# Loading the first six raw weight pieces from SyncE's queue instead of ScalarE's

## The chip, the cores and the metric

The kernel runs on one core of one Trainium2 chip. The metric is the device time of the whole program in microseconds (us), lower is better. Three runs of the kernel before gave 1136.29, 1137.8 and 1132.78 us; the median is 1136.29 us. All statements on where time goes come from one more execution, taken with the hardware profiler.

## The reference

The program is an attention block followed by two feed-forward blocks. Cut to what matters:

```python
# attention: 4 batches x 8 heads, 576 tokens, head size 64
scores = q @ k.T / 8
scores = where(scores >= max(scores) - tau, scores, -1e9)
attn = exp(scores - max(scores)); attn = attn / (sum(attn) + 1e-9)
x = (attn @ v) laid out as (2304, 512)
# first block: w_in 512 x 2048, w_out 2048 x 512
h = relu(x @ w_in); y = (s * h * h + b) @ w_out
# second block: same sizes, other weights
h2 = y @ w2_in; out = (h2 * tanh(log1p(exp(h2)))) @ w2_out
```

Inputs are float32, but the weights `w_in`, `w_out`, `w2_in` and `w2_out` reach the core as 64-bit floats, read as pairs of 32-bit words, and the kernel puts each number together from the two words itself.

## The kernel before

**Attention** works on 16 pairs of heads (4 batches x 4 pairs). A pair has 9 row tiles of 128 rows (`ti` 0 to 8). For each tile `scores` multiplies (S, L338), finds the maximum (`ns`, VectorE, L342) and takes the exponential (ScalarE, L349); later `weights_t` transposes the result on TensorE (T, L376) and ScalarE copies it out (`te`, L387); `products_v` multiplies with v (pv, L406); `split_x` (L414) cuts the pair's output into two parts, `self.x[pr]`.

The q and k of the next pair are prepared one pair ahead, in `prep_qk` (L294), k at `ti` 2 and q at `ti` 4. `raw_t` transposes the raw tile on TensorE and at once issues the load of the raw tile of the pair after (L250, L251). `parts` (L274) splits the transposed tile into a high part on ScalarE (`hik` or `hiq`, L278) and a low part on VectorE (`lok`, `loq`, L279). k and q share one buffer for the high part and one for the low. **Moves** then copy these parts between partitions into the operand tiles KH, KL and Q, as DMAs of 144 KB on SyncE's queue (L299): six for k, four for q. `self.moved` is the last move issued so far. So `hiq` can be written only when the moves that read `hik` have landed.

**Weight pieces.** `w_in` and `w_out` are cut into 32 pieces of 512 KB of raw words. `split_w` takes one piece through five steps: its load into a raw tile (L59, four buffers); nothing; a scaling on ScalarE in place (L65); three bit operations on VectorE (L67 to L69, two buffers); a rounded copy on ScalarE (L72) and a subtraction (L73). `split_all` starts one piece at each call and moves each live piece by one step. Finished pieces go into `ring` (five buffers) and are stored to DRAM (L194, SyncE's queue), to be read again for later batches. The marks `keep_in_program_order` on L59 and L65 keep these loads and scalings in the order of the program on ScalarE's queue.

`run` calls `split_all` (`next(w1)`) six times while `self.x[3]` doesn't exist yet, at steps 42, 52, 62, 72, 82 and 92 of the attention generator. These calls start pieces 0 to 5. During this stage the PSUM pool `self.s2p` is open; afterwards it is `None`. The remaining 26 pieces are started from `first()`, within the first block's work on batch 0 (`moe1(0)`: h and y, L503), interleaved with attention of pair 4 and on. Step 42 falls in pair 2 at `ti` 2, just after the k moves for pair 3 are traced; steps 52 and 62 come after the q moves for pair 3; steps 72 and 82 after the q moves for pair 4; step 92 after the q moves for pair 5.

**Order.** Each engine has one queue and runs it strictly in order. The order in a queue is set when the program is built, by a planner that simulates a timeline and may put an instruction ahead of others traced before it. A DMA is issued by the engine whose queue it is in: `nc.sync` is SyncE (SP), which does nothing else, and `nc.scalar` is ScalarE (ACT), which also does all the copies and exponentials. An issue that must wait holds up what stands behind it in that queue. `issue_after(i)` ties an instruction of the same engine behind instruction `i`.

Of the kernel before, what the change touches and what calls it, by code (L numbers as in the profile page):

```python
# [19 lines left out]
class Fused:  # L20
# [26 lines left out]
    def split_w(self, src, hi, lo, pool, tags, kw):  # L47

        nc = self.nc
        i = self.nd
        self.nd += 1
        n = src.shape[1] * src.shape[2] // 2
        raw = pool.tile([P, n, 2], I32, tag=tags[0], name=f"wraw{i}", **kw)
        self.tc.keep_in_program_order(nc.scalar.dma_start(raw.rearrange("p (c f) w -> p c (f w)", c=src.shape[1]), src))  # L59
        low, high = raw[:, :, 0], raw[:, :, 1]  # L60
        hf = high.bitcast(F32)
        yield
        yield
        a = pool.tile([P, n], I32, tag=tags[1], name=f"wa{i}")
        self.tc.keep_in_program_order(nc.scalar.activation(hf, hf, AF.Copy, scale=2.0 ** -112))  # L65
        yield
        nc.vector.tensor_scalar(a, high, 3, None, op0=ALU.logical_shift_left)  # L67
        nc.vector.scalar_tensor_tensor(a, low, 29, a, op0=ALU.logical_shift_right, op1=ALU.bitwise_or)
        nc.vector.scalar_tensor_tensor(a, high, -0x80000000, a, op0=ALU.bitwise_and, op1=ALU.bitwise_or)  # L69
        yield  # L70
        af = a.bitcast(F32).rearrange("p (c f) -> p c f", c=src.shape[1])
        nc.scalar.copy(hi, af)  # L72
        (nc.gpsimd if self.s2p else nc.vector).tensor_tensor(lo, af, hi.bitcast(F32), op=ALU.subtract)  # L73
# [863 lines left out]
```

## Time and profile before

| | us |
|---|---|
| median of three runs | 1136.29 |
| lowest, highest of the three | 1132.78, 1137.8 |
| the profiled execution, its own time | 1133.57 |
| its span (first to last instruction) | 1131.8 |
| TensorE (PE) busy | 1081.1 |
| VectorE (DVE) busy | 806.3 |
| ScalarE (ACT) busy | 619.0 |

Lines of a trace read so: start, duration, engine (SPq and ACTq are the issuing queues of SyncE and ScalarE), line of the kernel, operation, tile written <- tiles read, shapes, count, and in square brackets how long the engine sat idle before it and what ended that. Rows on DMA issues give the tile, the count, the size and the median us from issue to landing. Rows of stretches give, for each engine, busy us and the number of instructions, then the granted clock of TensorE as a share of full speed, the mean busy share of the 16 DMA engines, and GB/s.

### The profile page before, as it was taken

To read this page: it belongs to the slowest core of one execution; us is meant where nothing else is said; L and a number is where in the kernel's file an instruction comes from. 1 tells how busy PE (TensorE), PEld (TensorE's weight loads), DVE (VectorE), ACT (ScalarE), POOL (GpSimd) and SP (SyncE) were. 2 spreads that over 40 slices of the span, in tenths; PEclk is the share of its full clock that TensorE was granted. 3 is DMA by queue.
4 is the path that set the end of the run, shared out by engine and by line. 5 is a ranking of instruction groups with operands and counts; after the bars stand their busy time and mean duration, and the time that the engine had idled before them with its cause. 6 is when DMAs were issued, how large, how long until landed. Compare 5 with 4: busy or idle time off the path is not lost.

```text
span 1131.8 us, 21384 instructions
## 1 busy us (share of the span) xinstructions
PE 1081.1 (96%) x7964; PEld 1018.7 (90%) x7964; DVE 806.3 (71%) x1746; ACT 619.0 (55%) x1153; POOL 263.4 (23%) x306
## 2 busy tenths in 40 slices
PE   7887799999999999999999989999999999999998
PEld 6765599898999998888989879999999999999998
DVE  6987799999666677878866666735696368725782
ACT  4655497684576665667747557634363244513351
POOL 4533273351352442325334301100000000000000
PEclk9998899999999999999999999999999999999999
DMA  7366585966847869689864599977998999996683
GB/s 163 80 169 167 172 256 207 300 199 203 246 135 215 249 222 278 214 292 302 310 211 141 190 355 365 361 268 282 351 383 319 343 420 367 348 336 253 263 294 117
DMA packets 141591, 292.70 MB, mean 259 GB/s; under 512 B 52848, under 2 KB 78960, under 8 KB 133168
## 3 DMA queue, kind: packets, MB, share of 16 engines
q1 hardware_dynamic: 123408, 274.26, 70.8%
q10 hardware_dynamic: 18080, 17.07, 5.2%
q8 instruction: 63, 1.03, 0.4%
q14 instruction: 40, 0.33, 0.1%
HBM read 201.85 MB, written 66.58 MB: 237 GB/s over the span
## 4 chain that ended last, share of the span: by engine, by line
PE 67%; DVE 3%; DMA 3%; ACT 2%; issue 1%; POOL 0%; DVEq 0%; ACTq 0%; POOLq 0%
PE o L748 16%; PE y L503 13%; PE h L503 12%; PE qY L614 6%; PE qX L614 4%; PE qV L614 4%; PE S L338 3%; PE pv L406 3%; PE T L376 3%; DMA wso<-chlo 1%; DMA wi<-wsi 1%; PE pv L403 1%; PE T L381 1%; DMA w<-w 1%; ACT e L349 0%
## 5 line engine op out<-in xcount | busy, mean ns | idle before, releaser
L363 POOL TENSOR_SCALAR e<-e,st 128x576 f32<-128x576 f32 x128 | 133.4, 1055 | 229.0 <-DVE st L358 163.9
L748 PE MATMUL o<-wo,hl 128*128 128x256 f32 x1512 | 177.7, 279 | 0.0
L748 PEld LDWEIGHTS o<-wo,hl 128*128 128x128 f32 x1512 | 177.4, 188 | 0.0
L503 PE MATMUL y<-gh,w 128*128 128x288 f32 x768 | 165.0, 300 | 3.4 <-ACT y L548 1.7
L503 PE MATMUL h<-xh,w 128*128 128x288 f32 x768 | 164.7, 299 | 1.6 <-ACT xh L414 0.7
L342 DVE TENSOR_SCALAR_CACHE_REDUCE ns<-S 128x576 f32<-128x576 f32 x144 | 108.0, 752 | 53.6 <-PE S L338 53.2
L349 ACT ACTIVATE e<-ns,st 128x576 f32<-128x576 f32 x128 | 99.1, 776 | 64.4 <-DVE ns L342 62.0
L387 ACT COPY te<-T 128x576 f32<-128x576 f32 x144 | 91.8, 637 | 72.4 <-PE T L381 61.7
L353 DVE SCALAR_TENSOR_TENSOR e<-ns,st,e 128x576 f32<-128x576 f32 x128 | 114.9, 899 | 22.6 <-ACT e L349 21.6
L503 PEld LDWEIGHTS y<-gh,w 128*128 128x128 f32 x768 | 126.7, 189 | 4.5 <-ACT y L548 2.0
L503 PEld LDWEIGHTS h<-xh,w 128*128 128x128 f32 x768 | 125.8, 188 | 2.9 <-ACT xh L414 1.2
L527 POOL TENSOR_TENSOR gl<-rr,gh 128x288 fp32r<-128x288 f32 x96 | 93.6, 989 | 128.8 <-ACT rr L526 128.8
L503 PE MATMUL y<-gl,w 128*128 128x288 f32 x384 | 113.9, 297 | 0.9 <-POOL gl L527 0.9
L503 PE MATMUL h<-xl,w 128*128 128x288 f32 x384 | 113.5, 296 | 0.0
L338 PE MATMUL S<-KH,Q 128*128 128x288 f32 x320 | 97.2, 320 | 11.2 <-DVE lok L279 4.1
L376 PE MATMUL T<-ident,e 128*128 128x128 f32 x576 | 92.5, 283 | 15.3 <-ACT te L387 14.7
L376 PEld LDWEIGHTS T<-ident,e 128*128 128x128 f32 x576 | 68.7, 144 | 33.0 <-issue 18.0
L338 PE MATMUL S<-KL,Q 128*128 128x288 f32 x320 | 91.6, 302 | 0.0
L614 PE MATMUL qY<-yc,wi 128*128 128x384 f32 x432 | 86.6, 337 | 1.3 <-DVE g L637 1.3
L406 PE MATMUL pv<-te,rawv 128*64 128x288 f32 x576 | 86.6, 416 | 0.0
L614 PEld LDWEIGHTS qY<-yc,wi 128*128 128x128 f32 x432 | 75.6, 188 | 1.9 <-DVE g L637 1.9
L338 PEld LDWEIGHTS S<-KH,Q 128*128 128x128 f32 x320 | 62.3, 195 | 16.0 <-DVE ns L342 6.6
(150 smaller groups left out, 2204.4 us busy)
## 6 DMA issues: line engine op xcount, KB each, us to landing
w<-w SPq DMA_DIRECT2D x96, 512.0 KB, 5.1
wo<-wso SPq DMA_DIRECT2D x42, 1024.0 KB, 7.0
wi<-wsi SPq DMA_DIRECT2D x23, 1024.0 KB, 7.8
wi<-wsi SPq DMA_DIRECT2D x25, 768.0 KB, 7.4
w<-wp SPq DMA_DIRECT2D x32, 512.0 KB, 4.8
wsi<-chli SPq DMA_DIRECT2D x24, 512.0 KB, 5.1
wso<-chlo SPq DMA_DIRECT2D x24, 512.0 KB, 7.1
ycd<-yp SPq DMA_DIRECT2D x14, 768.0 KB, 8.1
```

The costliest lines, as they stand in the source:

```text
L338: self.scored = nc.tensor.matmul(so, Q[:, c0:c0 + 128], kt[:, ks], start=(i == 0), stop=(i == len(terms) - 1)).ins
L342: nc.vector.tensor_scalar(ns.rearrange("p (h n) -> p h n", h=2), sv, -0.125, 3.0e38, op0=ALU.mult, op1=ALU.min, accum_out=nm[:, c1])
L349: nc.scalar.activation(e, ns, AF.Exp, bias=nm[:, c1], scale=-1.0)
L353: nc.vector.scalar_tensor_tensor(e, ns, nthr[:, c1], e, op0=ALU.is_le, op1=ALU.mult, accum_out=sm[:, c1])
L363: nc.gpsimd.tensor_scalar(t, t, rinv[:, j:j + 1], u[:, j:j + 1], op0=ALU.mult, op1=ALU.add)
L376: nc.tensor.transpose(T[:, i * 128:i * 128 + 128], self.es[pr, i, "pair"][:, o:o + 128], self.ident)
L387: nc.scalar.copy(te, T[:, :576])
L406: ins = self.nc.tensor.matmul(*args, **kw).ins
L503: nc.tensor.matmul(acc[:, :n], w[:, wl, c], rhs[c][xl][:, ts], start=(i == 0), stop=(i == 11))
L527: (nc.vector if b == 3 else nc.gpsimd).tensor_tensor(gl[:, ts], r2, gh[:, ts].bitcast(F32), op=ALU.subtract)
L614: self.nc.tensor.matmul(acc, a, b, start=(first and i == 0), stop=(i == n - 1), skip_group_check=True)
L748: nc.tensor.matmul(bank[p][t], hl[:, gl, j, ts], w[:, 2 * (q % 2) + j, wl], start=(old is None and q + j + k == 0), stop=(q + j + k == 6), ...
```

## The change

In `split_w`, while `self.s2p` is open (pieces 0 to 5), the raw load is issued by SyncE, tied behind the latest move issued so far. From piece 6 on it is issued by ScalarE, as before.

```diff
@@ split_w
         raw = pool.tile([P, n, 2], I32, tag=tags[0], name=f"wraw{i}", **kw)
-        self.tc.keep_in_program_order(nc.scalar.dma_start(raw.rearrange("p (c f) w -> p c (f w)", c=src.shape[1]), src))
+        dst = raw.rearrange("p (c f) w -> p c (f w)", c=src.shape[1])
+        if self.s2p:
+            with self.tc.issue_after(self.moved):
+                nc.sync.dma_start(dst, src)
+        else:
+            self.tc.keep_in_program_order(nc.scalar.dma_start(dst, src))
         low, high = raw[:, :, 0], raw[:, :, 1]
```

## Rows read from the trace of the kernel before

**Rows 1.** Busy time of each engine over the span, from the page.
```profile
PE 1081.1 (96%) x7964; PEld 1018.7 (90%) x7964; DVE 806.3 (71%) x1746; ACT 619.0 (55%) x1153; POOL 263.4 (23%) x306
```

**Rows 2.** Stretches of 20 us: stretch, length, PE, PEld, DVE, ACT, POOL, clock, DMA.
```profile
40.00:60.00 20.00, 18.12 (x136) 14.01 (x136) 18.23 (x58) 12.61 (x19) 11.17 (x10) 1.00 0.45 102
...
100.00:120.00 20.00, 13.55 (x97) 10.52 (x94) 17.39 (x40) 12.85 (x22) 7.46 (x7) 0.95 0.94 257
120.00:140.00 20.00, 16.14 (x94) 11.22 (x93) 12.26 (x37) 7.83 (x12) 4.43 (x3) 0.79 0.43 126
140.00:160.00 20.00, 19.91 (x155) 19.21 (x154) 18.51 (x39) 18.25 (x41) 14.21 (x13) 1.00 0.76 217
```

**Rows 3.** Instructions on the raw weight tiles: duration in ns, min/median/max.
```profile
L67 DVE TENSOR_SCALAR wa<-wraw x32: 414/428/1093, 80.4 to 273.0; 128x512 int32<-128x512 int32 x32
L68 DVE SCALAR_TENSOR_TENSOR wa<-wraw,wa x32: 664/690/1327, 82.1 to 274.5; 128x512 int32<-128x512 int32 x32
L69 DVE SCALAR_TENSOR_TENSOR wa<-wraw,wa x32: 674/692/1749, 84.0 to 276.2; 128x512 int32<-128x512 int32 x32
L59 ACTq DMA_DIRECT2D wraw<-in_moe_w_in_dram x16: 374/375/520, 65.1 to 237.8; - x16
```

**Rows 4.** DMA issues of the stretches 56-60.9, 78.3-83 and 115-116 us.
```profile
KH<-hik SPq DMA_DIRECT2D x4, 144.0 KB, 2.8
...
KH<-hik SPq DMA_DIRECT2D x4, 144.0 KB, 6.7
...
rawq<-in_q_dram SPq DMA_DIRECT2D x1, 256.0 KB, 9.2
```

**Rows 5.** Timeline of all engines around the preparation for pair 4.
```profile
78.12 0.37 ACTq L59 DMA_DIRECT2D wraw<-in_moe_w_in_dram  x1
...
80.30 1.35 SPq L299 DMA_DIRECT2D KH<-hik  x2
...
83.95 0.78 ACT L349 ACTIVATE E<-ns,st 128x576 f32<-128x576 f32 x1 [0.63 <-DVE ns L342]
87.54 0.69 ACT L278 CAST hiq<-tpq 128x640 fp32r<-128x640 f32 x1 [2.81 <-DMA rawv<-in_v_dram]
...
88.83 1.11 PE L376 MATMUL T<-ident,e 128*128 128x128 f32 x4 [4.07 <-ACT te L387]
```

**Rows 6.** Timeline of PE a pair earlier, where no weight load was under way.
```profile
63.37 0.95 PE L376 MATMUL T<-ident,e 128*128 128x128 f32 x4 [2.29 <-ACT te L387]
```

**Rows 7.** Timeline of all engines around the preparation for pair 5.
```profile
101.39 0.93 ACTq L59 DMA_DIRECT2D wraw<-in_moe_w_in_dram  x2
...
106.53 0.38 ACTq L59 DMA_DIRECT2D wraw<-in_moe_w_in_dram  x1
...
115.04 0.65 SPq L250 DMA_DIRECT2D rawq<-in_q_dram  x1
...
118.36 1.23 SPq L299 DMA_DIRECT2D Q<-loq  x2
...
124.32 0.41 ACTq L59 DMA_DIRECT2D wraw<-in_moe_w_out_dram  x1
...
124.77 0.64 ACT L387 COPY te<-T 128x576 f32<-128x576 f32 x1 [3.07 <-DMA rawq<-in_q_dram]
...
125.47 1.11 PE L376 MATMUL T<-ident,e 128*128 128x128 f32 x4 [2.82 <-ACT te L387]
...
128.06 4.69 PE L406 MATMUL pv<-te,rawv 128*64 128x288 f32 x21
...
129.07 0.69 DVE L69 SCALAR_TENSOR_TENSOR wa<-wraw,wa 128x512 int32<-128x512 int32 x1
```

**Rows 8.** Stretches of 4 us, columns as in rows 2.
```profile
72.00:76.00 4.00, 4.00 (x33) 3.14 (x29) 3.29 (x14) 1.33 (x3) 1.97 (x3) 1.00 0.00 0
...
128.00:132.00 4.00, 4.00 (x20) 2.04 (x18) 2.88 (x8) 0.92 (x2) 3.67 (x3) 0.52 0.19 66
```

**Rows 9.** The chain that ended last, one piece: start, us, what.
```profile
265.84 2.43 PE pv L406 x21
```

## The prediction

> **What bounds the kernel now.** First the busy times: TensorE is busy for 96% of the span [rows 1], so what can be won is the little that it idles or runs slowly. Then the stretches of 20 us, to see where that is. From 140 us on TensorE is busy for all of 20 us at full clock; in the stretch from 100 to 120 us for 13.55 of 20, and from 120 to 140 us for 16.14 at a granted clock of 0.79. Attention without any weight work, from 40 to 60 us, has 18.12 at full clock [rows 2]. So the stage to read is that from 60 to 140 us, in which attention runs alone on TensorE and the six loads of the change fall. A stall removed there should reach the end, because behind it TensorE is nearly full: what it does later just starts earlier.
>
> In that stage I looked for TensorE's longest idle times and followed each back. There are two.
>
> *Stall A, pair 4.* TensorE waits 4.07 us, up to 88.83, for `te`, a copy on ScalarE. ScalarE itself stood still for 2.81 us ahead of `hiq` at 87.54 [rows 5]. `hiq` reuses the buffer of `hik`, so it waits for the k moves that read `hik`. The row names a load of v as releaser; by the buffers and by time it is the last KH move: the pair of issues at 80.30 lasts 1.35 us, so the second starts at about 81.0, and with the 6.7 us from issue to landing of that stretch it lands at 87.7, within 0.2 us of the start of `hiq`. A round earlier, with no weight load in flight, the same four moves took 2.8 us [rows 4]. What is different is the load of piece 2, issued by ScalarE at 78.12, 2 us ahead of these moves [rows 5].
>
> *Stall B, pair 5.* The loads of pieces 3 and 4 go out together at 101.39, that of piece 5 at 106.53 [rows 7]. From then to about 124 us the DMA engines have almost no pause: their mean busy share is 0.94 from 100 to 120 us [rows 2], and the raw q load issued at 115.04 needs 9.2 us [rows 4], so it lands at 124.24. ScalarE's next load is issued at 124.32, 0.1 us after that, and the `te` copy behind it starts at 124.77, after 3.07 us of idle time that the trace puts down to that q load [rows 7]. Nothing of the copy depends on it. Between the q load and this issue lie seven other DMAs (one more raw q, a weight load, four moves, a store). So I read it as a limit of eight DMAs under way for the program's two queues: the issue waits for the one eight places back. TensorE loses 2.82 us, up to 125.47, and then runs a batch of 21 products of `pv` in 4.69 us [rows 7] where the same batch takes 2.43 us elsewhere [rows 9]; the granted clock of that stretch is 0.52 [rows 8], about the lower of the two levels, 1.2 GHz, after idle time.
>
> **The change, part by part.** *Six issues leave ScalarE.* Each holds its queue for 0.375 us [rows 3], 2.25 us in all. ScalarE is busy 7.83 to 12.85 us in 20 in this stage [rows 2], and the queue is idle beside it; I take 0. Bounds: 2.25 us gained if each fell on the path, 0 lost.
>
> *Six issues join SyncE.* They stand behind the moves. Loads 1 and 2 stand behind the q moves for pair 3 which are issued in the few us after the transposition of rows 6; I estimate 67 us for the loads. Load 2 goes out at 78.12 today [rows 5]. The DMA engines have nothing at all to do from 72 to 76 us [rows 8], so loads issued at 67 have room to land before the k moves for pair 4. Loads 3 and 4 go behind the q moves for pair 4, which follow `hiq` of 87.54 [rows 5] by a few us: about 91, an estimate, instead of 101.39; load 5 goes behind those for pair 5, so from 106.53 to about 119.6, the end of the q moves that start at 118.36 [rows 7]. Load 0, at 65.1 today [rows 3], may go a few us earlier, behind the k moves for pair 3. What is queued behind a load on SyncE is the next raw load and the next moves, and stores of finished pieces. A load that must wait for a buffer would hold these: load 4 reuses the buffer of piece 0, whose last bit operation starts at 84.0 [rows 3], 7 us ahead; load 5 that of piece 1, long free by 119. I take 0. Load 0 may stand ahead of the q load and q moves for pair 3 in the same queue, and make them land later: at most by the 6.7 - 2.8 = 3.9 us that a load cost the k moves [rows 4]. It falls among these q moves today too, so I take 0; bounds 0 and 3.9.
>
> *Stall A.* With load 2 out of the way the k moves should take 2.8 us instead of 6.7: the last one issued at about 81.0 lands at 83.8 to 84.4, before ScalarE is through with its last exponential, at 83.95 + 0.78 = 84.7 [rows 5]. So the whole 2.81 us of idle time of ScalarE goes [rows 5]. Of TensorE's 4.07 us, 1.26 us stay, from the chain hiq, te that runs anyway. Bounds: 0, if another wait is late next, and 2.81; I take 2.8. TensorE's clock also falls after stall A, up to about 94 us, but it fell too after the 2.29 us of idle time a pair earlier [rows 6], so I claim nothing for it; upper bound 2.7 us, half of the 5.3 us from 88.83.
>
> *Stall B.* Pieces 3 and 4 (1 MB) leave the crowded stretch altogether, piece 5 leaves its beginning. The q load should then land some us earlier, before the next weight load is issued: if it is lengthened like the moves were, by 3.9 us or more, that is by 120.3 instead of 124.2. I take the whole 2.82 us, and with them the slow `pv` batch, 4.69 - 2.43 = 2.26 us, since without idle time before it I see no reason for the lower clock. Bounds: 0 (ScalarE still issues loads 6 to 8 in this stretch, and these can meet the same limit) and 5.1.
>
> *What is late next.* Weight work of VectorE itself is not reduced, and VectorE is busy 17.39 of 20 us from 100 to 120 [rows 2]. Pieces 1 to 4 have to be split there unless the planner spreads them; I claim nothing for that, with an upper bound of 4 us.
>
> Sum: 2.8 + 2.82 + 2.26 = 7.9 us off. The profiled execution has 1133.57 us, its span of 1131.8 and 1.8 around it, so it would come to 1125.7. It lies 2.7 us under the median, 1136.29; on the scale of the median the forecast is 1128.4 us, 0.7% less. A measurement of this kernel can tell about 0.5% (5.7 us) from no change.
>
> **A rule that speaks against it.** The rows of stall A show a load on ScalarE's queue lengthening moves on SyncE's. The Trainium skill, "DMA: Bandwidth & Descriptors", section "Issuing engines are not separate DMA queues", says that DMAs of all issuing engines run on the same 16 DMA engines and interleave, and that issuing from several saves only the time of the issue. The trace agrees on the interleaving: 6.7 against 2.8 us [rows 4]. By that rule alone the choice of the queue is worth nothing, and only the moment of issue counts; this is the third rival below.
>
> **The rivals.** *Only A goes.* Loads 6 to 8 stay on ScalarE's queue, and load 7 stands behind the scaling of piece 5, which now waits for a later load. Then ScalarE meets a wait in the same place (load 5 issued at about 119.6, plus some us), and stall B with its slow batch stays. For it: the issue that waited at 124.32 isn't one of the six. Against it: 1.5 MB less DMA work before it. Time: 1136.29 - 2.8 = 1133.5.
>
> *Slower: the split of pieces 5 and 6 slides into the next stage.* Load 5 is 13 us later; piece 6's scaling and loads 7 and 8 are held in order behind piece 5's scaling on ScalarE. Today VectorE is through with the bit operations of both pieces at 129.8 us [rows 7]. If their start slips past 140 us they fall where VectorE is busy 18.51 of 20 us and TensorE all of it [rows 2]. Price: two pieces by 0.43 + 0.69 + 0.69 [rows 3] is 3.6 us, and a slow clock behind the stall, as in stall A, 2.7; together 6.3. It decides from the point where piece 5's bit operations start after 140 us, and it is slower than before if it also takes the place of A and B: 1142.6. Against it: load 5, issued at about 119.6, lands by about 126 even if it takes the moves' 6.7 us, with 14 us to spare, in which VectorE has room (12.26 of 20 busy from 120 to 140).
>
> *Nothing happens.* The planner leaves scaling and splits where they are, or issues the loads late on SyncE again, so that they meet the next k moves as today; the moment of issue, not the queue, is what counts. Time: 1136.3.
>
> **How the numbers follow.** Chances: forecast 0.45, only A 0.25, slower 0.18, nothing 0.12. The likeliest, 1128.4, is the predicted time. Its own range goes from the bounds of what I left out: down 2.7 for the clock after A and 4 for VectorE, to 1121.7; up to about 1133 where B goes only in part. The range for 8 in 10 leaves out the worst part of the slower case: 1121.5 to 1141. Faster by over 0.5% (under 1130.6): most of the forecast's case and a little of the second, 0.44. Slower by over 0.5% (over 1142): a good part of the slower case, and an unlucky order of the planner later on, 0.17. Within: 0.39.
>
> **What would show it.** Right: the KH moves for pair 4 land in about 3 us; `hiq` of pair 4 shows no idle time over 1 us ahead of it; weight loads 1 and 2 appear on SyncE's queue before 70 us; no `te` copy waits behind a weight load around 115 to 125 us; pair 3's output, and the stretch from which TensorE stays full (140 us today), comes 6 to 8 us earlier; from there on the stretches look as before. Wrong: the k moves still take 6 us; a raw load or a move on SyncE stands behind a weight load; the bit operations of piece 5 start after 140 us; or pair 3's output comes earlier and the end doesn't, which would mean that the planner's later order gave it back.

## The result

The changed kernel takes 1124.13 us (median; 1123.92 to 1125.02), beside 1134.67 us for the kernel before in the same comparison: a ratio of 0.9904, interval 0.9881 to 0.9927, so 0.7 to 1.2% less. The profiled execution takes 1124.25 us with a span of 1122.5 us, 9.3 us less than the span of before. The forecast was 7.9 us less, 1128.4, with a range from 1121.5 to 1141. The change is faster, as forecast; but TensorE's waiting time at stall B hardly shrank, and the order of TensorE's work brought something that no term had.

Busy time of the engines, from the page of the changed kernel (compare [rows 1]):

```profile
PE 1074.1 (96%) x7964; PEld 1012.1 (90%) x7964; DVE 803.1 (72%) x1746; ACT 618.7 (55%) x1153; POOL 261.6 (23%) x306
```

TensorE runs the same 7964 products in 7.0 us less. Its idle time, span less busy, falls by only 2.3 us, from 50.7 to 48.4. So in this pair of profiles most of the gain is shorter busy time, not less waiting. The stretches of the changed kernel (columns as in [rows 2]):

```profile
100.00:120.00 20.00, 13.01 (x92) 9.68 (x90) 19.98 (x48) 13.65 (x22) 4.82 (x5) 1.00 0.76 199
120.00:140.00 20.00, 16.93 (x122) 12.61 (x122) 15.55 (x45) 11.24 (x19) 8.27 (x9) 1.00 0.44 148
140.00:160.00 20.00, 19.87 (x155) 19.42 (x155) 19.50 (x35) 18.95 (x45) 12.79 (x12) 1.00 1.03 292
```

From 100 us on the granted clock is 1.00 throughout, where it was 0.95 and 0.79. The DMA engines' share from 100 to 120 us falls from 0.94 to 0.76. VectorE now is busy for 19.98 of 20 us there.

The clock differs from run to run as well. The 70 comparable runs of the kernel before in the experiments have a mean granted clock of 0.988 over the whole program, the 16 of the changed kernel 0.994. At 0.994 four runs of the kernel before take 1127.6 to 1131.4 us and three of the changed kernel 1123.9 to 1126.2. So far as these seven runs tell, some 4 us of the gain are there at the same clock, and the rest goes with the clock.

Stall A. DMA issues of the changed kernel during the k moves for pair 4 (77.7 to 81.5 us), then during the q load for pair 5 (111.4 to 113 us); below them ScalarE's and TensorE's timeline:

```profile
KH<-hik SPq DMA_DIRECT2D x4, 144.0 KB, 2.8
...
rawq<-in_q_dram SPq DMA_DIRECT2D x1, 256.0 KB, 3.8
```

```profile
84.65 0.69 ACT L283 CAST hiq<-tpq 128x640 fp32r<-128x640 f32 x1 [1.94 <-DMA KH<-hik]
...
86.60 0.66 PE L381 MATMUL T<-ident,e 128*128 128x128 f32 x4 [2.19 <-ACT te L392]
```

The k moves take 2.8 us in the median, as forecast, instead of 6.7 [rows 4]; `hiq` comes 2.9 us earlier and TensorE waits 2.19 us instead of 4.07 [rows 5]. The trace now names the KH move itself as what ended the wait. The four transpositions behind it take 0.66 us instead of 1.11.

Stall B. ScalarE and SyncE of the changed kernel around the load of piece 5, then TensorE:

```profile
115.90 0.46 ACTq L64 DMA_DIRECT2D wraw<-in_moe_w_out_dram  x1
116.00 0.58 SPq L62 DMA_DIRECT2D wraw<-in_moe_w_in_dram  x1
...
122.82 0.67 ACT L70 ACTIVATE wraw<-wraw 128x512 f32<-128x512 f32 x1 [4.11 <-DMA wraw<-in_moe_w_in_dram]
```

```profile
119.89 0.40 PE L508 MATMUL h<-xh,wp 128*128 128x288 f32 x1 [0.93 <-DVE ns L347]
...
124.06 0.46 PE L408 MATMUL pv<-te,rawv 128*64 128x288 f32 x1 [1.52 <-ACT te L392]
...
124.36 2.35 PE L411 MATMUL pv<-te,rawv 128*64 128x288 f32 x17
```

The wait of the `te` copy behind a load [rows 7] is gone. In its place ScalarE waits 4.11 us ahead of the scaling of piece 5, for a load that was issued at 116.0. TensorE has h products to run in that gap, from 119.89 on (18 of them, which ran at 133 us before), and idles for 1.52 us only. The `pv` batch runs at full clock: 17 of its products in 2.35 us.

### The profile page after: what moved, and what is told of

It is laid out like the page before. It is cut to its first block, busy times and chain, and to the rows that moved or that the text cites. A ratio compares the mean times of both kernels' runs of the same rounds, so it can differ in the third digit from the quotient of the medians.

```text
span 1122.5 us, 21392 instructions
## 1 busy us (share of the span) xinstructions
PE 1074.1 (96%) x7964; PEld 1012.1 (90%) x7964; DVE 803.1 (72%) x1746; ACT 618.7 (55%) x1153; POOL 261.6 (23%) x306
## 4 chain that ended last, share of the span: by engine, by line
PE 75%; DVE 8%; DMA 7%; ACT 5%; issue 3%; POOL 2%; SPq 1%; ACTq 0%; DVEq 0%; POOLq 0%
PE o L753 16%; PE y L508 15%; PE h L508 13%; PE qY L619 6%; PE S L343 5%; PE pv L411 4%; PE T L381 4%; PE qX L619 4%; PE qV L619 4%; DMA w<-w 2%; DVE e L358 1%; PE pv L408 1%; POOL e L368 1%; DMA wi<-wsi 1%; DVE ns L347 1%
```

## The experiments

The kernel before ran beside each kernel on the same chip; ratios are to it. Theory: two stalls, A and B, both made by a weight load beside DMAs that ScalarE waits for, directly or through the limit on DMAs under way. Rivals: the issue slots of ScalarE; and an order of the planner that happens to be better.

### The changed kernel again, and its two halves

> The changed kernel again, on the chip on which the next three run. Every theory expects what it gave before, about 0.990 of the kernel before (1124 us against 1135).

Measured: 0.992 (0.9901 to 0.9939).

Only pieces 0 to 2 moved:

```diff
-        if self.s2p:
+        if i < 3:
             with self.tc.issue_after(self.moved):
```

> Only pieces 0 to 2 are loaded from SyncE's queue behind the moves, pieces 3 to 5 from ScalarE's queue as before. Theory (two separate stalls, A by the load of piece 2 among the k moves for pair 4, B by the loads of pieces 3 to 5): stall A goes and B stays. The k moves for pair 4 take about 2.8 us, hiq of pair 4 comes 2.5 to 3 us earlier, the q load for pair 5 still needs about 9 us, TensorE's clock still falls between 116 and 132 us; 2.5 to 3.5 us less than before, ratio about 0.9975. Rival (issue slots of ScalarE): half of the whole gain, 5 us, ratio 0.995, by three issues as by the other three. Rival (the order of the planner, by luck): no relation, anything from 0.990 to 1.

Measured: 0.9974 (0.9951 to 0.9998). Profile of this kernel: the q load for pair 5 among the DMA issues, then the timeline of ScalarE and TensorE:

```profile
rawq<-in_q_dram SPq DMA_DIRECT2D x1, 256.0 KB, 8.7
```

```profile
86.41 0.69 ACT L283 CAST hiq<-tpq 128x640 fp32r<-128x640 f32 x1 [1.88 <-DMA KH<-hik]
...
121.29 0.38 ACTq L64 DMA_DIRECT2D wraw<-in_moe_w_out_dram  x1
121.71 0.64 ACT L392 COPY te<-T 128x576 f32<-128x576 f32 x1 [2.90 <-DMA rawq<-in_q_dram]
...
122.40 1.11 PE L381 MATMUL T<-ident,e 128*128 128x128 f32 x4 [2.83 <-ACT te L392]
...
125.00 4.32 PE L411 MATMUL pv<-te,rawv 128*64 128x288 f32 x21
```

`hiq` comes 8.0 us after `hik`, as in the changed kernel (8.1), where it was 10.3: A is gone. B stands: q load of 8.7 us, `te` behind a load, a slow `pv` batch.

Only pieces 3 to 5 moved:

```diff
-        if self.s2p:
+        if 3 <= i < 6:
             with self.tc.issue_after(self.moved):
```

> Only pieces 3 to 5 are loaded from SyncE's queue behind the moves, pieces 0 to 2 from ScalarE's queue as before. Theory (two separate stalls): A stays, with k moves for pair 4 of 6 to 7 us and hiq of pair 4 near 87.5 us; B goes, the q load for pair 5 lands in under 5 us and the clock doesn't fall between 116 and 132 us; 6 to 8 us less than before, ratio 0.993 to 0.995. Rival (issue slots of ScalarE): 5 us, ratio 0.995, the same as with the first three. Rival (planner's luck): no relation.

Measured: 0.9946 (0.9924 to 0.9967). Profile of this kernel: the k moves for pair 4 and the q load for pair 5 among the DMA issues, then `hiq` of pair 4 in the timeline:

```profile
KH<-hik SPq DMA_DIRECT2D x4, 144.0 KB, 6.4
...
rawq<-in_q_dram SPq DMA_DIRECT2D x1, 256.0 KB, 3.8
```

```profile
87.84 0.69 ACT L283 CAST hiq<-tpq 128x640 fp32r<-128x640 f32 x1 [2.86 <-DMA rawv<-in_v_dram]
```

Here A stands and B is gone. The two halves are 0.26% and 0.54%, together 0.80%, and the whole was 0.80 to 0.96%. Each half takes away its own stall and leaves the other; the second half holds also what the order of TensorE's work gives, to which a section below comes. Equal halves of 0.45%, as the issue slots would have it, lie within both intervals, so the times alone don't exclude them; the rows and the next two runs do.

### The traffic, and the issue slots, put back

Extra loads from ScalarE's queue where the weight loads stood before, beside the six on SyncE's queue; first of full size, then of 4 KB:

```diff
         if self.s2p:
+            extra = pool.tile([P, n, 2], I32, tag="extra", name=f"extra{i}", bufs=1)
+            self.tc.keep_in_program_order(nc.scalar.dma_start(extra.rearrange(...), src))
             with self.tc.issue_after(self.moved):
                 nc.sync.dma_start(dst, src)
```

> The changed kernel with six more loads of 512 KB, into a tile that nobody reads, issued by ScalarE where the weight loads stood before: the traffic among the moves is back, the weights themselves come as in the changed kernel. Theory (traffic beside the moves): the k moves for pair 4 take 6 to 7 us again, hiq of pair 4 comes near 87 us, stall A is back whole and B at least in part: 4 to 10 us over the changed kernel, 1128 to 1135. Rival (the gain is from the earlier arrival of the weights or the planner's order): as the changed kernel, 1123 to 1126.

Measured: 1.000 (0.9973 to 1.0027). The whole gain is gone, and stall A is back: `hiq` comes 10.6 us after `hik`. DMA issues around the k moves for pair 4 (the median of the four issues hides that the last ones take up to 7.2 us), then ScalarE and TensorE:

```profile
KH<-hik SPq DMA_DIRECT2D x4, 144.0 KB, 5.4
extra<-in_moe_w_in_dram ACTq DMA_DIRECT2D x1, 512.0 KB, 7.1
```

```profile
88.48 0.69 ACT L285 CAST hiq<-tpq 128x640 fp32r<-128x640 f32 x1 [2.89 <-DMA rawv<-in_v_dram]
...
89.77 1.09 PE L383 MATMUL T<-ident,e 128*128 128x128 f32 x4 [4.14 <-ACT te L394]
```

Stall B is not back: only three extra loads fall between 101 and 112 us, and the q load for pair 5 lands in under 4 us. Part of the loss was made by the experiment itself. All extra loads share one buffer, so each waits for the one before it; the fifth lands at 111.19 us, the sixth is issued at 111.21 on ScalarE's queue, and ScalarE stands still for 3.94 us ahead of what comes behind it:

```profile
111.21 0.45 ACTq L62 DMA_DIRECT2D extra<-in_moe_w_in_dram  x1
111.70 0.64 ACT L421 CAST xh<-pv 128x576 fp32r<-128x576 f32 x1 [3.94 <-PE S L345]
```

TensorE's order is that of the kernel before, too (see below). So this run shows what makes stall A, and its 1.000 is not the price of the traffic alone.

> As the run with six extra full loads, but each extra load has only 4 KB: the issue on ScalarE's queue is back, the traffic isn't. Theory (traffic beside the moves): k moves for pair 4 of about 2.8 us, no stall A, within 2 us of the changed kernel. Rival (issue slots of ScalarE, or its waits for one of eight DMAs under way): ScalarE stands still ahead of these issues, 4 to 10 us over the changed kernel, like the full loads.

Measured: 0.9947 (0.9919 to 0.9974). The issues alone bring neither stall back; DMA issues around the k moves for pair 4, then `hiq`:

```profile
KH<-hik SPq DMA_DIRECT2D x4, 144.0 KB, 3.6
extra<-in_moe_w_in_dram ACTq DMA_DIRECT2D x1, 4.0 KB, 3.2
```

```profile
84.74 0.69 ACT L285 CAST hiq<-tpq 128x640 fp32r<-128x640 f32 x1 [1.72 <-DMA KH<-hik]
```

These two kernels have the same order of TensorE's work. So it is the bytes under way beside the moves, not the place in ScalarE's queue, that made stall A. This is what the rule that the prediction weighed asks for: by the Trainium skill, "DMA: Bandwidth & Descriptors", section "Issuing engines are not separate DMA queues", DMAs of all engines interleave on the same 16 DMA engines. The trace agrees, with 3.6 us for the moves beside the small loads and 5.4 beside the full ones.

Stall B came back in neither run: that the loads of pieces 3 to 5 make it is shown by the two halves, and that it is by their bytes is argued from the rows. And 0.9947 is not the 0.990 to 0.992 of the changed kernel: 3 to 5 us stay open at this point, where the expectation was 2 at most. They come up again below.

### The queue without the tie to the moves

```diff
-            with self.tc.issue_after(self.moved):
-                nc.sync.dma_start(dst, src)
+            nc.sync.dma_start(dst, src)
```

> All six loads from SyncE's queue, but not tied behind any move: the planner may put them anywhere. It puts four of them near the start of the program, one between the q moves for pair 4, one behind the k moves for pair 5. Theory (what counts is that no load is under way beside the moves on which ScalarE waits): the k moves for pair 4 take 2.8 us and stall A goes; four loads of 2 MB at the start lengthen the first moves, at 14 to 25 us, and cost 0 to 4 us there; together 1124 to 1129. Rival (the tie behind the moves is what brings the gain): near the kernel before, 1132 to 1136.

Measured: 1.0013 (0.9983 to 1.0043). The six loads leave ScalarE's queue here too, and nothing is won. TensorE's two longest waits in the profile of this kernel:

```profile
30.86 0.61 PE L342 MATMUL S<-KH,Q 128*128 128x288 f32 x1 [4.36 <-DVE loq L283]
...
100.47 0.58 PE L342 MATMUL S<-KH,Q 128*128 128x288 f32 x1 [4.08 <-DMA Q<-loq]
```

The four loads at the start of the program delay the moves for pair 1; the load between the q moves for pair 4 delays their second half, and the scores wait for it. Stall A is gone, as expected (7.1 us from `hik` to `hiq` of pair 4). The theory expected a part of the gain, 1124 to 1129 us; it had priced the first new stall too low, at 0 to 4 us (pair 0's output comes at 59.46 us instead of 52.96), and overlooked the second. TensorE's order is that of the kernel before here as well. The queue alone wins nothing; where its loads stand does.

### All loads, or an earlier load of piece 5

```diff
-        if self.s2p:
+        if True:
```

> All 32 loads from SyncE's queue behind the latest moves. Theory (the first stage is where the loads meet the moves that ScalarE waits on): the first stage as in the changed kernel, pair 3's output near 134.5 us; then each load of the later pieces waits on SyncE behind stores and moves of a pair that come only every 40 us, so pieces run late: TensorE idles between 140 and 290 us, and the time is 5 to 40 us over the changed kernel. Rival (SyncE's queue is better for all loads): as the changed kernel or less, 1120 to 1125.

Measured: 1.0102 (1.0049 to 1.0154), 1144.4 us. Pair 3's output comes at 132.0 us, but in the stage from 140 to 300 us TensorE runs only 1085 products in 147.36 us, so the early lead is lost and more:

```profile
140.00:300.00 160.00, 147.36 (x1085) 135.06 (x1084) 116.02 (x291) 105.76 (x209) 54.44 (x77) 0.96 0.62 194
```

Piece 5 tied behind the k moves for pair 5 (`moved_k` is the last of these), not its q moves:

```diff
-            with self.tc.issue_after(self.moved):
+            with self.tc.issue_after(self.moved_k if i == 5 else self.moved):
```

> All six loads from SyncE's queue, but that of piece 5 tied behind the k moves for pair 5 and not behind its q moves. In the changed kernel ScalarE waits 4.1 us, up to 122.8, for this load. Theory (that wait costs what its length is): the load goes out near 109 us, ScalarE's wait is gone, and the time falls by another 1 to 4 us, to 1120 to 1123. Rival (the wait is hidden by the early h products that TensorE runs in it): no change, 1123 to 1125. Rival (the load now stands ahead of the q load and q moves for pair 5, and a stall like B comes back): 1126 to 1130.

Measured: 0.9956 (0.9932 to 0.9979), 1128.2 us. The time is that of the third expectation: the load stands ahead of the q load for pair 5, which takes 8.2 us, and ScalarE waits 3.05 us still (DMA issues, then timeline). But this kernel has the order of before in TensorE's later work (see below), worth some 3 us by itself; from `hik` of pair 5 to pair 3's output it takes only 0.8 us more than the changed kernel. So the time doesn't show what the load costs there.

```profile
rawq<-in_q_dram SPq DMA_DIRECT2D x1, 256.0 KB, 8.2
```

```profile
115.31 0.67 ACT L70 ACTIVATE wraw<-wraw 128x512 f32<-128x512 f32 x1 [3.05 <-DMA wraw<-in_moe_w_in_dram]
```

### Pieces 6 and 7 behind the same moves

```diff
         if self.s2p:
-            with self.tc.issue_after(self.moved):
+            self.early = self.moved
+        if i < 7:      # i < 8 in the second kernel
+            with self.tc.issue_after(self.early):
                 nc.sync.dma_start(dst, src)
```

> The changed kernel, with piece 6 as well loaded from SyncE's queue, tied behind the q moves for pair 5 as piece 5 is. In the changed kernel the loads of pieces 5 and 6 go out together, at 116.0 and 115.9 us from two queues, and ScalarE waits 4.1 us for piece 5. Theory (that wait is the load of piece 6 beside that of piece 5, and costs): piece 5 lands 1 to 2 us earlier, the wait falls to 2 to 3 us, pair 3's output comes 1 to 2 us earlier and the time falls to 1121 to 1124. Rival (the wait is covered by early h products): within 2 us of the changed kernel. Rival (piece 6 is late for the first y products): 1126 to 1132.

> As the run with piece 6, and piece 7 too from SyncE's queue behind the q moves for pair 5; by the planner's order it stands behind one store. Theory (a load on ScalarE's queue may hold ScalarE): one more issue leaves ScalarE, no more than 1 us beside the run with piece 6 alone, 1120 to 1124. Rival (SyncE's queue gets full: the stores and the next raw k load wait behind a load that waits for its buffer): 1 to 6 us over the changed kernel.

> The changed kernel again on the chip of the two runs beside it, for the comparison with them: about 0.991 of the kernel before.

Measured: 0.9885 (0.9855 to 0.9915) with piece 6, 0.9888 (0.9856 to 0.9921) with pieces 6 and 7, 0.9916 (0.9888 to 0.9944) for the changed kernel beside them. With piece 6 behind piece 5 in one queue, piece 5 lands in 4.9 us instead of 6.8 and ScalarE's wait falls from 4.11 to 2.22 us (DMA issues, then timeline):

```profile
wraw<-in_moe_w_in_dram SPq DMA_DIRECT2D x1, 512.0 KB, 4.9
```

```profile
121.26 0.68 ACT L72 ACTIVATE wraw<-wraw 128x512 f32<-128x512 f32 x1 [2.22 <-DMA wraw<-in_moe_w_in_dram]
```

The wait behaves as expected. The time is 0.3% less than the changed kernel's, but the intervals overlap: a gain is not shown.

### The order of TensorE's work

The stretch of 140 to 300 us in the kernel before, then in the changed kernel:

```profile
140.00:300.00 160.00, 157.17 (x1210) 147.15 (x1209) 146.44 (x332) 114.96 (x233) 71.98 (x85) 1.00 0.75 231
```

```profile
140.00:300.00 160.00, 159.45 (x1237) 149.55 (x1237) 142.65 (x336) 113.40 (x229) 67.87 (x82) 1.00 0.77 243
```

The same for every kernel but that with all loads on SyncE's queue, beside four stretches in us from start to start in the timelines: from `hik` to `hiq` of pair 4 (stall A on ScalarE), from `hik` of pair 4 to `hik` of pair 5 (the round with stall A), from there to pair 3's output (with stall B), and from pair 3's output to pair 4's:

| kernel | `hik` to `hiq` | round of A | stretch of B | pair 3's to pair 4's output | products, 140-300 |
|---|---|---|---|---|---|
| before | 10.30 | 25.34 | 37.59 | 38.93 | 1210 |
| first three moved | 7.97 | 22.50 | 35.80 | 38.89 | 1209 |
| full extra loads | 10.59 | 24.72 | 34.95 | 38.88 | 1210 |
| small extra loads | 7.80 | 22.62 | 33.08 | 38.88 | 1212 |
| without the tie | 7.06 | 26.99 | 31.22 | 39.03 | 1207 |
| piece 5 earlier | 7.60 | 22.16 | 35.24 | 38.89 | 1211 |
| changed | 8.07 | 23.41 | 34.43 | 37.73 | 1237 |
| changed, second profile | 7.57 | 22.35 | 34.39 | 37.71 | 1235 |
| changed, third profile | 7.72 | 22.28 | 34.23 | 37.71 | 1236 |
| last three moved | 10.30 | 25.49 | 34.43 | 37.69 | 1236 |
| piece 6 too | 7.64 | 22.18 | 33.02 | 37.71 | 1236 |
| pieces 6 and 7 too | 7.97 | 22.51 | 33.01 | 37.70 | 1237 |
| two full extra loads (below) | 7.32 | 23.65 | 34.35 | 37.71 | 1236 |

One cell doesn't fit the theory: with the first three pieces moved, the stretch of B takes 1.8 us less than before, though the slow q load, the wait of `te` and the slow batch are all there. Why stays open.

In the second stage no load of the change is left, and yet TensorE runs either about 1210 products in it or about 1236, and a pair takes either 38.9 or 37.7 us. The kernel before and the five below it in the table form one group, the changed kernel and the rest the other. In the traces the order of TensorE's 7964 products, by the tiles that each writes and reads, falls into the same two groups: each kernel agrees to 99% or more with the kernel before, or with the changed kernel, and to 92 or 93% with the other of the two. The planner, which sees where the loads stand, lays out two different orders. One more run separates order from traffic, with two full extra loads that leave the order as it is in the changed kernel:

```diff
         if self.s2p:
+            if i in (3, 4):
+                extra = pool.tile([P, n, 2], I32, tag="extra", name=f"extra{i}", bufs=1)
+                self.tc.keep_in_program_order(nc.scalar.dma_start(extra.rearrange(...), src))
             with self.tc.issue_after(self.moved):
```

> The changed kernel with two extra loads of 512 KB, into a tile that nobody reads, issued by ScalarE beside those of pieces 3 and 4. By the instruction streams TensorE's order is that of the changed kernel, not that of the kernel before, which the six extra loads brought back. Theory (the stage from 140 to 300 us gains by TensorE's order, whatever the traffic was before it): about 1236 products in that stage, as in the changed kernel, and not 1210; the traffic costs 0 to 4 us ahead of 140 us; ratio to the kernel before 0.992 to 0.996. Rival (that stage gains by the lighter traffic): about 1210 products in it and a ratio of 0.996 to 1.

Measured: 0.9939 (0.9917 to 0.9962). The extra traffic is there, the q load for pair 5 takes 5.4 us instead of 3.8, and the second stage keeps its products, and its pair of 37.7 us:

```profile
140.00:300.00 160.00, 159.48 (x1236) 149.05 (x1234) 142.34 (x336) 112.62 (x227) 67.58 (x82) 1.00 0.78 243
```

So the second stage goes with TensorE's order, not with the loads ahead of it. 26 products more at 160 us for 1236 are 3.4 us.

## Why the prediction was right, and where it wasn't

**Stall A: the mechanism was right and the size nearly, the account of what stays was not.** Forecast 2.8 us. From `hik` to `hiq` of pair 4 the three profiles of the changed kernel take 8.1, 7.6 and 7.7 us where it was 10.3: 2.2 to 2.7 us less. The rounds of A take 1.9, 3.0 and 3.1 us less. In the first of these profiles, beside the same stretch of before, 1.3 of the 1.9 us are idle time and 0.6 are busy time for the same 141 products at a higher clock (columns as in [rows 2]), for which the prediction claimed nothing:

```profile
77.24:102.58 25.34, 20.48 (x141) 16.73 (x138) 19.36 (x58) 14.03 (x23) 8.86 (x10) 0.87 0.59 154
```

```profile
76.58:99.99 23.41, 19.88 (x141) 15.94 (x138) 19.76 (x60) 13.82 (x23) 8.27 (x10) 0.93 0.63 169
```

The step that failed: "the whole 2.81 us of idle time of ScalarE goes". 1.94 us of it stay, for two reasons. The 2.8 us are the median of four moves, and the last one is waited for: it takes 4.3 us, and it took 3.9 in the round of before from which the 2.8 were read. And the exponential which ran ahead of `hiq` at 83.95 before stands behind it now, at 85.24: ScalarE idles where it ran, and the `te` copy for which TensorE waits comes 1.27 us after `hiq` began instead of 0.59. DMA issues at 58.0 to 58.7 us before and at 80.2 to 80.9 us after, then ScalarE after:

```profile
KH<-hik SPq DMA_DIRECT2D x1, 144.0 KB, 3.9
```

```profile
KH<-hik SPq DMA_DIRECT2D x1, 144.0 KB, 4.3
```

```profile
85.24 0.78 ACT L354 ACTIVATE E<-ns,st 128x576 f32<-128x576 f32 x1
85.92 0.63 ACT L392 COPY te<-T 128x576 f32<-128x576 f32 x1
```

The first three pieces alone gave 0.26%, 3.0 us, with an interval from 0.2 to 5.6.

**Stall B: right that it goes, too large by two fifths.** Forecast 5.1 us: 2.82 of waiting and 2.26 of a slow batch. Measured from `hik` of pair 5 to pair 3's output 3.2 us (3.2 and 3.4 in the other two profiles), first before, then after:

```profile
102.58:140.17 37.59, 27.28 (x168) 19.71 (x167) 29.58 (x75) 19.45 (x31) 9.50 (x8) 0.86 0.73 203
```

```profile
99.99:134.42 34.43, 24.55 (x172) 17.49 (x171) 30.77 (x81) 20.30 (x33) 8.35 (x9) 1.00 0.67 192
```

TensorE's busy time falls by 2.7 us, with four products more, at a clock of 1.00 instead of 0.86; its idle time falls by 0.4 only. So the term of the clock was about right. It had been sized by a piece of the chain, 2.43 us [rows 9]; in the timeline of before the same 21 products take 2.83 us at full clock, a pair earlier, so the batch alone was worth 1.86 us, and other products of the stretch gained the rest:

```profile
70.32 2.83 PE L406 MATMUL pv<-te,rawv 128*64 128x288 f32 x21
```

The step that failed is the other term: "I take the whole 2.82 us", with nothing taken off for the wait that is late next. TensorE's waits in the two stretches (total us, times, longest), first before, then after:

```profile
PE T L376 <- ACT te L387: 6.0, 4, 2.8
PE S L338 <- DVE ns L342: 1.2, 2, 0.9
PE pv L403 <- ACT te L387: 0.7, 1, 0.7
```

```profile
PE S L343 <- DVE ns L347: 2.7, 5, 1.1
PE T L381 <- ACT te L392: 2.4, 3, 1.5
PE pv L408 <- ACT te L392: 1.5, 1, 1.5
PE h L508 <- DVE ns L347: 0.9, 1, 0.9
```

Waits for ScalarE's `te` fall by 2.8 us, from 6.7 to 3.9, as forecast; waits for the maximum `ns` on VectorE rise by 2.4, from 1.2 to 3.6. VectorE has the same weight work to do in a shorter stretch (30.77 us busy of 34.43, before 29.58 of 37.59), and is late next. A wait of ScalarE that the sum had at zero is in these numbers too: piece 5 lands at 122.8 and its scaling holds ScalarE for 4.11 us. The prediction had this wait in its first rival, with the outcome that B would stay whole. It didn't, since the h products cover the gap: TensorE's idle time there is 1.52 us and its clock doesn't fall.

**What no term had: TensorE's order later on.** 26 to 27 products more between 140 and 300 us, 3.4 us, go with the planner's order, as the last run points to: traffic back, order kept, products kept. The prediction named the planner's later order only as a risk, on the slow side. With 1.9, 3.2 and 3.4 the sum is 8.5 of the 9.3 us; 0.7 us lie ahead of `hik` of pair 4. They are no effect of the change: 0.4 of them are there at pair 0's output (52.96 to 52.55), ahead of every load, and in the other two profiles of the changed kernel `hik` of pair 4 comes 0.8 and 0.9 us later than before. The order alone was not timed with everything else equal. The small extra loads, which have the old order and little of the old traffic, are at 0.9947 beside 0.990 to 0.992; that is the size, but the intervals overlap.

**The signs.** Pair 3's output comes 5.8 us earlier, a little less than the 6 to 8 that were to show the forecast right; `hiq` has 1.94 us of idle time ahead of it instead of 1 at most; and the stretches behind 140 us do not look as before. The other signs of being right came true. One of being wrong came true as well, without a cost that shows: on SyncE's queue the load of piece 0, at 62.73, stands ahead of the raw q load of 63.41, which takes 6.5 us instead of 4.6 before; `hik` of pair 4 is no later for it in this profile.

**The rivals.** The split of pieces 5 and 6 does not slide past 140 us: VectorE takes piece 5's first bit operation at 123.5. SyncE's queue was not held by a load that waits for its buffer, in the changed kernel; with all 32 loads it was (that run's trace has 12.7 us of such waits). That the moment counts and not the queue, the third rival's reason, is borne out here, and speaks for the change: the untied loads on the same queue gave 1.0013.

**The total was right partly by luck:** A and B together gave 5.1 us in the first profile of the changed kernel and 6.2 and 6.4 in the others, 1.5 to 2.8 less than forecast, against 3.4 us that nobody asked for.

## What to carry to other kernels

When an engine waits for a small DMA, look what large DMA was issued just ahead of it on any queue, and compare the landing times with a round that has none: 6.7 against 2.8 us told the cause of stall A here. Tying a load that has time to spare behind the moves that do not was worth it here; the queue alone wasn't. Size such a stall by the last landing, not the median, and by what is late behind it: at stall B 2.4 of the 2.8 us came back as waits for another engine. And give a rearranged schedule a term of its own on both sides: here about a third of the gain goes with it.

## What the runs showed of the hardware

Two loads of 512 KB issued 0.1 us apart from two queues need 6.1 and 6.8 us (the changed kernel, 115.9 and 116.0); put into one queue, 0.6 us apart, the first lands in 4.9 and the second in 5.8 (with piece 6 too, 116.4 and 117.0).

Issues waited for the DMA eight places back: before, 124.32 against a q load that lands at 115.04 + 9.2 = 124.24 [rows 4, 7]; with the first three pieces alone, 121.29 against one issued at 112.55, which lands 8.7 us later, at 121.25. The traces say where the eight comes from: in all 14 of them the program tells of the landing of its DMAs by eight semaphores used in turn, no issue finds more than seven other DMAs under way, and the issue at 124.32 has the semaphore of that q load. So it is a limit of these programs; whether the chip would take more DMAs at once, no run shows.
